# Attention, then two expert layers, on one core: a fixed order to the last pair, a spread gate chain, 32 products of constants

## Chip, cores and metric

One NeuronCore of a Trainium2 chip runs the whole program as one launch. The metric is the time of one execution in microseconds on the device. Three runs of the kernel before gave 632.25, 638.49 and 640.03 us; their median is 638.49 us.

## The reference, cut to what matters

```python
# q, k, v: 2 batches, 8 heads, 768 tokens, 64 per head; 4 sink keys; a window of 128
scores = scale * (q @ k.T)                      # kept: own 128-token window, and the sink keys
a = softmax(scores); x = (a @ v) as 1536 rows of 512
# first expert layer: 8 experts, the two best of each token, 512 -> 1024 -> 512
noisy = x @ w_gate + log1p(exp(x @ w_noise)) * noise
x = sum over the two best e of weight_e * (relu(x @ w1[e]) @ w2[e])
# second expert layer: 8 experts, the best of each token, with a bias by modality
out = prob_e * (relu(x @ w1b[e]) @ w2b[e])
```

## The kernel before, in words

**Attention.** The 1536 tokens are 12 tiles of 128 tokens. A tile has four pairs of heads, so there are 48 pairs, and the main loop (L1040) runs over pairs, j = 0 to 56, as a software pipeline written out by hand. In step j it issues the scores of pair j (`s_mm`, L406: 12 products of 128 columns in f16, 6 in the first tile of a batch, into one of two PSUM buffers named `s`), the row maxima of pair j-1 on DVE (`maxima`, L412 and L417), the exponentials of pair j-2 on ACT (L425), the turns of pair j-3 on TensorE (`pt_mm`, L431), and the products with V of pair j-7 (`pv`, L461, 8 products in f32). Other steps of a tile are put at a fixed number of pairs after its first one by a table (`put`, `fill`): the sink keys (L472, L503, L510, L516), the division by the row sums (`fin_x`, L535 and L537, which need the last products of the tile, L522), the split into two f16 halves (L547, L551), the turn of the row (L558 by DMA; for the last tile of a group, tiles 5 and 11, by eight products of TensorE, L562, and a copy on ACT, L563) and its gate logits (`lg_mm`, L568). The f16 splits of the first two experts' weights (L111 to L122) are put in between in the same way.

**Gating.** The tiles form two groups, 0 to 5 and 6 to 11. When the logits of a group are there, `gate_ops` (L574) makes a list of small operations, its gate chain (nearly all recorded as L609, the line of the helper `op`): noise, two best experts of each token (`max`, `max_index`), counts on TensorE (L647 to L650), ranks, then the slot lists: `lo` (128 x 1536), `ct` (128 x 1152), `ct` times the token numbers, and `place` (L702, 12 products). The chain of the first group ends in `ahead`, which gathers the rows of the first two experts' first blocks (L936) and appends their work to `todo` (four empty steps, then two turns L894, sixteen steps of the first layer L799, eight of the second L817, two that write rows). The chain of the second group ends in `gather1` (L763).

The chain's list holds marks, `BAR`. `drip` takes the next operation of the list unless it is a mark, and `tick` does so n times and then takes one mark away if it stands first. `maxima` drips `rate` operations at each of three places, `fin_x` two, and each step of the loop ends with a `tick` (L1082). So at most one section between marks is issued in a step:

```python
        rate[:], late_ticks, early_ticks = (DR, DR), TI if j < nu else PRM['TD'], 0
```

With DR 3 and TI 20, the first group's chain enters its list in step 38 and issues one whole section a step: step 39 has 29 operations (noise to the two best experts), step 45 has `lo`, `ct` and `ct` times tokens, step 46 `place`, step 47 the lists and `ahead`.

**Order.** Up to step MC the program order is the order on each engine (TensorE, DVE, ACT, POOL and the DMA queue of SP; `manual_schedule`, closed at L1042). After it a scheduler picks, for each engine, the next instruction at compile time from its own model of durations, with program order as priority. MC is 29, so 19 of the 48 pairs lie behind it. In program order `sink_p2` (L510) of a tile stands seven steps after the tile's first one, behind that step's scores, turns and products with V.

**Behind attention.** The work of `todo` is issued by a loop after the main loop, beside the second group's chain; then come the rest of experts 0 and 1 (L1411 to L1421, first product of `layer1(0)`: L799 with 288 columns), experts 2 to 7, and the second expert layer.

Of the kernel before, what the change touches and what calls it, by code (L numbers as in the profile page):

```python
# [1 line left out]
PRM = {"cuts": [0, 6, 12], "CP": 0, "BARS": 1, "DR": 3, "TI": 20, "TD": 30, "GW": 4, "JB": 50, "JN": 1, "TK": 4,  # L2
# [3 lines left out]
       "JP": 0, "XP": 0, "ptev": 5, "parts": 6, "max": 1, "finx": 10, "ptmm": 3, "exps": 2, "finsum": 9, "pv": 7,  # L6
# [33 lines left out]
def attention_moe_moe(ctx, tc, qk, v, n_sink, window, small, w1, w2, modality_id, modality_bias, w1b, w2b, out, CAP=416):  # L40
    nc = tc.nc
    V, A, G, T, S = nc.vector, nc.scalar, nc.gpsimd, nc.tensor, nc.sync
# [24 lines left out]
    cuts = PRM['cuts']  # L67
# [88 lines left out]
    sink = ps.tile([128, 512], FT, name="sink", bufs=1)  # L156
# [29 lines left out]
    ident = consts.tile([128, 128], HF, name="ident")  # L186
    tri = consts.tile([128, 128], HF, name="tri")
    ones = consts.tile([128, 128], HF, name="ones")
# [385 lines left out]
    def gate_ops(gi, ts, l):  # L574
# [31 lines left out]
        def op(f, *a, **kw):  # L606
            def run():
                with tc.high_priority(offset=CP):
                    f(*a, **kw)  # L609
            ops.append(run)  # L610
# [81 lines left out]
        def each(x, m):  # L692
            return x.rearrange("p c k -> p (c k)")[:, None, :].to_broadcast([128, m, 2 * n])

        op(V.tensor_tensor, lo, steps2[:, :, 0:2 * n], each(rh[:, 0], 128), op=OP.is_equal)
        op(V.tensor_tensor, ct, steps2[:, 0:NCOL, 0:2 * n], each(rh[:, 1], NCOL), op=OP.is_equal)
        op(V.tensor_tensor, ct, ct, each(tok1[:, t0:t0 + n], NCOL), op=OP.mult)
        bar()

# [229 lines left out]
    CP = PRM['CP']  # L929
# [69 lines left out]
    def tick(n):  # L999
        drip(n)  # L1000
        for c in chains:
            if c and c[0] is BAR:
                c.pop(0)
# [36 lines left out]
    for j in range(END):  # L1040
        if j == MC:
            man.close()  # L1042
        rate[:], late_ticks, early_ticks = (DR, DR), TI if j < nu else PRM['TD'], 0
        if early_ticks:
            tick(early_ticks)
        if j < nu:
            s_mm(*units[j])
        for h in range(2):
            k = j - PRM['finmm'] - 2 * h
            if k % 4 == 0 and 0 <= k // 4 < NT:  # L1050
                fin_mm(k // 4, h)
        k = j - PRM['ptev']
        if k % 2 == 0 and 0 <= k < nu:
            pt_ev(units[k][0], units[k][1] // 2)
        k = j - PRM['parts']
        if k % 2 == 0 and 0 <= k < nu:
            pt_parts(units[k][0], units[k][1] // 2)
        k = j - PRM['max']
        if 0 <= k < nu:
            maxima(*units[k])  # L1060
        for h in range(2):
            k = j - PRM['finx'] - 2 * h
            if k % 4 == 0 and 0 <= k // 4 < NT:
                fin_x(k // 4, h)
        k = j - PRM['ptmm']
        if 0 <= k < nu:
            pt_mm(*units[k])
        k = j - PRM['exps']
        if 0 <= k < nu:
            exps(*units[k])  # L1070
        for h in range(2):
            k = j - PRM['finsum'] - 2 * h
            if k % 4 == 0 and 0 <= k // 4 < NT:
                fin_sum(k // 4, h)
        k = j - PRM['pv']
        if 0 <= k < nu:
            pv(*units[k])
        if j >= JOBS:
            for _ in range(JN):
                step()  # L1080
        filled(j)
        tick(late_ticks)  # L1082
    ov = consts.tile([1, 2, E + 1], I32, name="ov")
    ovf = consts.tile([1, 2, E + 1], FT, name="ovf")
    at.close()
# [298 lines left out]
    j = END  # L1384
# [350 lines left out]
```

## Time and profile before

| | |
|---|---|
| three runs | 632.25, 638.49, 640.03 us; median 638.49 |
| the profiled execution | 641.03 us, its span 639.3 us |
| TensorE busy | 584.5 us (91%), mean granted clock 0.936 |
| DVE, ACT, POOL busy | 378.7 (59%), 301.8 (47%), 247.3 us (39%) |
| HBM | 142 GB/s over the span |

Times in the trace are microseconds from the start of the span. A granted clock of 1.00 is 2.4 GHz, one of 0.50 is 1.2 GHz. An instruction is named by its engine and by its line (L406 is line 406 of the kernel before).

### The profile page before, as it was taken

Reading aid. Unit: us, or ns where it says so; the run is one execution under the profiler, and the core shown is the slowest. Engines: PE = TensorE matmul, PEld = TensorE weight load, DVE = VectorE, ACT = ScalarE, POOL = GpSimd, SP = SyncE. Lnnn points to the kernel's source line nnn. Section 1 sums busy time; section 2 is a strip of 40 time slices with the busy share of each in tenths; the row PEclk is TensorE's granted clock in tenths of the full one; section 3 lists DMA queues with packets and bytes.
Section 4 is the critical chain, followed back from the end, with each engine's and each line's share of the span. In section 5 each row is a group of like instructions: output and inputs, shape, how many; then the busy total and the mean of one; then the engine's idle time right before and its main releaser. Section 6 shows DMA issues by size and latency. Waiting matters only on the chain. (4 is left out here: it accounts for less than half of the span.)

```text
span 639.3 us, 13126 instructions
## 1 busy us (share of the span) xinstructions
PE 584.5 (91%) x4764; PEld 407.5 (64%) x4764; DVE 378.7 (59%) x1036; ACT 301.8 (47%) x656; POOL 247.3 (39%) x274
## 2 busy tenths in 40 slices
PE   5699989799989999999999999999999697989982
PEld 4699888688867765555555555555545573755761
DVE  8799957934835848464747563356686572473420
ACT  6469857743234847454647463233452341452210
POOL 6577754432141354243341606042312381262210
PEclk9789968857899999999999999999999899889988
DMA  6778975447028578477584506017619865489320
GB/s 211 226 227 218 268 213 149 102 133 246 19 81 210 207 237 261 124 248 175 177 247 166 124 3 154 9 59 277 194 69 338 249 157 134 149 275 215 105 66 9
DMA packets 101048, 107.61 MB, mean 168 GB/s; under 512 B 62579, under 2 KB 65939, under 8 KB 100950
## 3 DMA queue, kind: packets, MB, share of 16 engines
q1 hardware_dynamic: 90102, 76.06, 42.9%
q0 software_dynamic: 9792, 28.26, 13.1%
q10 hardware_dynamic: 1056, 2.10, 0.9%
q8 instruction: 47, 0.77, 0.5%
q14 instruction: 51, 0.42, 0.2%
HBM read 76.03 MB, written 14.74 MB: 142 GB/s over the span
## 5 line engine op out<-in xcount | busy, mean ns | idle before, releaser
L799 PEld LDWEIGHTS <-w1s 128*128 128x128 f16 x1632 | 149.5, 102 | 85.6 <-issue 17.3
L799 PE MATMUL pp<-xtt,w1s 128*128 128x416 f16 (+2 forms) x864 | 152.3, 332 | 1.8 <-issue 1.0
L817 PE MATMUL pp<-hh,w2s 128*128 128x416 f16 (+2 forms) x960 | 141.4, 307 | 0.7 <-DVE hh L802 0.6
L817 PEld LDWEIGHTS <-w2s 128*128 128x128 f16 x960 | 87.7, 99 | 50.1 <-issue 1.0
L751 POOL DMA_INDIRECT yrow<-xga,ids x34 | 36.7, 1079 | 123.7 <-ACT xga L876 118.7
L825 DVE SCALAR_TENSOR_TENSOR yt<-pp,yt 64x416 f16<-64x416 f32 (+1 forms) x64 | 35.5, 555 | 65.2 <-ACT yt L823 58.4
L801 ACT ACTIVATE hh<-pp 128x416 f16<-128x416 f32 (+3 forms) x87 | 38.5, 461 | 57.8 <-PE pp L799 50.5
L802 DVE SCALAR_TENSOR_TENSOR hh<-pp,hh 128x416 f16<-128x416 f32 (+3 forms) x87 | 44.4, 518 | 32.3 <-ACT hh L801 22.7
L823 ACT ACTIVATE yt<-pp 64x416 f16<-64x416 f32 (+1 forms) x64 | 31.0, 485 | 68.1 <-PE pp L817 61.4
L122 DVE SCALAR_TENSOR_TENSOR w1s<-wf,w1s 128x1024 f16<-128x1024 f32 (+1 forms) x49 | 54.3, 1119 | 13.5 <-ACT w1s L115 10.0
L1539 PEld LDWEIGHTS <-hh 128*128 128x128 f16 x336 | 32.6, 98 | 37.9
L122 DVE SCALAR_TENSOR_TENSOR w2s<-wf,w2s 128x1024 f16<-128x1024 f32 (+1 forms) x43 | 52.6, 1262 | 3.3 <-ACT w2s L115 2.8
L461 PE MATMUL po<-vf,ptm 128*128 128x65 f32 x320 | 53.1, 319 | 0.6 <-issue 0.4
L1539 PE MATMUL po<-w2s,hh 128*128 128x512 f16 x240 | 52.8, 379 | 0.0
L461 PEld LDWEIGHTS po<-vf,ptm 128*128 128x128 f32 x320 | 51.2, 241 | 1.9 <-issue 1.2
L115 ACT ACTIVATE w1s<-wf 128x1024 f16<-128x1024 f32 (+1 forms) x51 | 45.6, 924 | 10.6 <-DMA wf<-in_moe_w_dram 5.0
L406 PEld LDWEIGHTS <-w2s 128*128 128x128 f16 x528 | 39.2, 113 | 14.2 <-issue 6.0
L115 ACT ACTIVATE w2s<-wf 128x1024 f16<-128x1024 f32 (+1 forms) x52 | 46.4, 918 | 0.9 <-remote 0.6
L763 POOL DMA_INDIRECT xg<-xrow,idg x30 | 30.2, 1008 | 29.0 <-DVE dst L609 20.1
L802 DVE SCALAR_TENSOR_TENSOR hh<-ph,hh 128x256 f16<-128x256 f32 (+1 forms) x48 | 17.2, 377 | 38.7 <-ACT hh L801 35.8
L406 PE MATMUL s<-w1s,w2s 128*128 128x128 f16 x264 | 31.4, 258 | 7.7 <-DVE w1s L348 5.4
L801 ACT ACTIVATE hh<-ph 128x256 f16<-128x256 f32 (+1 forms) x48 | 15.7, 347 | 46.7 <-PE ph L799 43.4
(304 smaller groups left out, 832.2 us busy)
## 6 DMA issues: line engine op xcount, KB each, us to landing
wf<-in_moe_w_dram SPq DMA_DIRECT2D x44, 1024.0 KB
w1s<-in_qk_dram SPq DMA_DIRECT2D x12, 512.0 KB
vf<-in_v_dram SPq DMA_DIRECT2D x12, 260.0 KB
xrow<-xr SPq DMA_DIRECT2D x12, 256.0 KB
w2s<-xga SPq DMA_DIRECT2D x22, 128.0 KB
wf<-in_moe_w_dram ACTq DMA_DIRECT2D x2, 1024.0 KB
yrow<-xga,ids POOLq DMA_INDIRECT x34
xtt<-xg SPq DMA_TRANSPOSE x31
```

Source lines behind the costliest of these rows:

```text
L115: A.activation(t[:, 0][:, o[0], o[1]], i, AF.Copy, scale=1.0 if v else SW)
L122: V.scalar_tensor_tensor(t[:, 1][:, o[0], o[1]], i, SW, h, op0=OP.mult, op1=OP.subtract)
L406: T.matmul(PS[t, p][:, c, j], head(t, a, 2 * p + j), KH[t - c][:, b, p // 2 * 2 + j], start=(j + a + b + c == 0), stop=(a > 0 and c == n - ...
L461: T.matmul(o[:, 2 * pp + j], x[:, 2 * pp + j], VV[t - c][:, 2 * p + j], start=(pp + j + c == 0), stop=(i == 0 and j + pp == 2), skip_group ...
L751: return G.indirect_dma_start(out=dst, out_offset=bass.IndirectOffsetOnAxis(ap=idx, axis=0), in_=src, in_offset=None, bounds_check=n - 1, ...
L799: ordered(1, T.matmul(p[:, :n], wa[:, a, d, fs], x[:, c * KD + d, r], start=(k_ == 0), stop=(k_ == len(passes) - 1)))
L801: A.activation(hh[:, 0, f, q], p[:, :n], AF.Relu)
L802: V.scalar_tensor_tensor(hh[:, 1, f, q], p[:, :n], 0.0, hh[:, 0, f, q], op0=OP.max, op1=OP.subtract)
L817: ordered(2, T.matmul(p[:, :n], wt[:, a, f, dd], hh[:, c, f, q], start=(k_ == 0), stop=(k_ == len(passes) - 1)))
L823: A.activation(y[s, 2 * d + x, r], p[s, :n], AF.Copy, scale=z)
L825: V.scalar_tensor_tensor(y[hs[1 - x], 2 * d + x, r], p[s, :n], z, y[s, 2 * d + x, r], op0=OP.mult, op1=OP.subtract)
L1539: T.matmul(p[:m], hh[:, c, f, o:o + m], wb[:, a, f], start=(f == 0 and k_ == 0), stop=(f == KF - 1 and k_ == 2))
```

## The change

Three parameters change: DR from 3 to 1, TI from 20 to 3, and MC from 29 to 48. Two marks are added between the three large operations of the first group's chain; the second group's chain, the last one, gets none there. Thirty-two products of two constants are issued at the end of step 47, into columns of the tile `sink` that nothing reads.

```diff
-PRM = {... "DR": 3, "TI": 20, ...
-       "MC": 29, ...
+PRM = {... "DR": 1, "TI": 3, ...
+       "MC": 48, ...
...
         op(V.tensor_tensor, lo, steps2[:, :, 0:2 * n], each(rh[:, 0], 128), op=OP.is_equal)
+        bar(gi < len(groups) - 1)
         op(V.tensor_tensor, ct, steps2[:, 0:NCOL, 0:2 * n], each(rh[:, 1], NCOL), op=OP.is_equal)
+        bar(gi < len(groups) - 1)
         op(V.tensor_tensor, ct, ct, each(tok1[:, t0:t0 + n], NCOL), op=OP.mult)
         bar()
...
         filled(j)
         tick(late_ticks)
+        if j == nu - 1:
+
+            for _ in range(32):
+                T.matmul(sink[:, 384:512], ones, ident, start=True, stop=True)
```

With one operation at each of the three places of `maxima` and three in the `tick`, a step issues six operations of the chain, eight where `fin_x` stands (every second step). Counted through the list: the section of 29 takes steps 40 to 44, the next three sections steps 45, 46 and 47, the product of the totals step 48, the ranks step 49 (behind the last pair the `tick` has 30 operations), `lo`, `ct` and the product with the tokens steps 50, 51 and 52, `place` 53, and the lists with `ahead` 54.

## Rows read from the trace of the kernel before

**Rows 1.** The page's 40 slices: granted TensorE clock in tenths of full speed
```profile
PEclk9789968857899999999999999999999899889988
```
**Rows 2.** Windows by stage: stretch, length, busy us (instructions) by engine, clock, DMA
```profile
67.96:83.28 15.32, 13.35 (x181) 12.02 (x180) 12.94 (x55) 12.46 (x39) 11.54 (x13) 1.00 1.07 296
83.28:102.03 18.75, 18.75 (x158) 17.44 (x157) 8.93 (x42) 9.29 (x30) 7.06 (x9) 0.54 0.68 165
102.03:119.72 17.69, 16.09 (x205) 13.97 (x204) 17.57 (x85) 13.61 (x39) 11.97 (x16) 1.00 0.40 113
119.72:125.23 5.51, 3.16 (x26) 2.68 (x27) 5.51 (x12) 4.41 (x11) 1.44 (x2) 0.93 0.73 183
125.23:146.76 21.53, 21.53 (x133) 19.17 (x130) 9.85 (x35) 9.37 (x23) 7.16 (x9) 0.50 0.43 118
146.76:185.44 38.68, 33.53 (x525) 31.51 (x525) 22.21 (x103) 12.75 (x47) 8.86 (x8) 0.89 0.36 113
```
**Rows 3.** Windows, L406 alone: the score products, 12 to a pair
```profile
67.96:83.28 15.32, 5.96 (x84) 4.97 (x83) 1.00 1.07 296
83.28:102.03 18.75, 7.20 (x60) 6.52 (x60) 0.54 0.68 165
102.03:119.72 17.69, 5.17 (x72) 4.28 (x72) 1.00 0.40 113
```
**Rows 4.** Windows: two stretches at half clock, and one at full
```profile
83.50:100.57 17.07, 17.07 (x146) 15.98 (x143) 7.67 (x34) 8.02 (x25) 6.84 (x9) 0.50 0.65 150
124.46:151.77 27.31, 27.31 (x203) 24.79 (x202) 14.58 (x46) 11.78 (x32) 9.79 (x11) 0.50 0.49 142
...
36.00:83.50 47.50, 44.92 (x580) 40.35 (x577) 42.99 (x164) 39.50 (x120) 36.90 (x46) 1.00 0.88 242
```
**Rows 5.** Timeline of TensorE before the first fall: start, length, instruction, [idle before]
```profile
83.11 0.24 PE L510 MATMUL sink<-ident,sks 128*64 128x128 f16 x1 [1.40 <-POOL sks L503]
83.29 0.23 PE L406 MATMUL s<-w1s,w2s 128*128 128x128 f16 x1
```
**Rows 6.** Timeline of TensorE around the second fall
```profile
117.82 1.00 PE L461 MATMUL po<-vf,ptm 128*128 128x65 f32 x8
...
119.73 0.84 PE L406 MATMUL s<-w2s 128*128 128x128 f16 x12 [0.41 <-DVE mx L417]
...
123.14 2.28 PE L702 MATMUL misc<-ct,lo 128*128 128x96 f16 x12 [2.34 <-DVE ct L609]
125.24 1.46 PE L406 MATMUL s<-w2s 128*128 128x128 f16 x12
126.50 1.91 PE L461 MATMUL po<-vf,ptm 128*128 128x65 f32 x8
```
**Rows 7.** Timeline of DVE there
```profile
119.60 0.99 DVE L609 TENSOR_TENSOR ct<-steps,rh 128x1152 f16<-128x1152 f16 x1
...
121.38 1.71 DVE L609 TENSOR_TENSOR ct<-ct,tok 128x1152 f16<-128x1152 f16 x1
```
**Rows 8.** Timeline of TensorE, the turn and the logits of tile 5
```profile
93.76 1.01 PE L562 MATMUL s<-ident,xr 128*128 128x128 f16 x8
...
96.30 0.51 PE L568 MATMUL misc<-wg,xt 128*128 128x16 f16 x12
```
**Rows 9.** Timeline of ACT, the copy between them
```profile
94.81 1.01 ACT L563 COPY xt<-s 128x1024 f16<-128x1024 f16 x1 [2.58 <-PE s L562]
```
**Rows 10.** Groups of DVE, 100 to 130 us: first chain; count, busy us, mean ns
```profile
L609 DVE SCALAR_TENSOR_TENSOR gw<-gw 128x48 f32<-128x48 f32 x8 | 4.4, 553 | 0.0
```
**Rows 11.** The same group, 158 to 174 us: second chain
```profile
L609 DVE SCALAR_TENSOR_TENSOR gw<-gw 128x48 f32<-128x48 f32 x8 | 1.6, 205 | 0.2
```
**Rows 12.** Timeline of TensorE, the second chain's last count
```profile
165.66 0.17 PE L650 MATMUL misc<-acum,ones 128*128 128x8 f16 x1
```
**Rows 13.** Timeline of POOL: first gathers of the first and of the second chain
```profile
126.36 1.21 POOL L936 DMA_INDIRECT xga<-xrow,idga  x1 [3.89 <-DVE mx L417]
...
173.28 0.99 POOL L763 DMA_INDIRECT xg<-xrow,idg  x1 [20.12 <-DVE dst L609]
```

More of the change, by code (lines that the diff above doesn't have):

```diff
@@ L1 @@
 import math
-PRM = {"cuts": [0, 6, 12], "CP": 0, "BARS": 1, "DR": 3, "TI": 20, "TD": 30, "GW": 4, "JB": 50, "JN": 1, "TK": 4,
[1 row of a table removed]
+PRM = {"cuts": [0, 6, 12], "CP": 0, "BARS": 1, "DR": 1, "TI": 3, "TD": 30, "GW": 4, "JB": 50, "JN": 1, "TK": 4,
[1 row of a table added]
        1, "direct": 1, "OT": 2, "S3": 0, "SK": 1, "SL": 0, "LS": 2, "L0": 2, "LN": 3, "LW": 12, "EN": 9, "xs": 128,
```

2 rows, old and new, of the table PRM are left out of this document.

## The prediction

> **What bounds the kernel now.** I read the slices of the granted clock first, because TensorE is the busiest engine and its clock is what varies: the row is 8 or 9 nearly everywhere, but 6 in the sixth slice (80 to 96 us) and 5 in the ninth (128 to 144) [rows 1]. Then the windows. Two long stretches run at 0.50, that is 1.2 GHz: 83.50 to 100.57 and 124.46 to 151.77 [rows 4]. In both TensorE is busy all the time (17.07 of 17.07, 27.31 of 27.31), so the lower clock there is paid in full: at 2.4 GHz the same products would take about half, 8.5 and 13.7 us less.
>
> The stage windows put this against the work [rows 2], and the score products alone count the pairs [rows 3]: 84 products are seven pairs, 60 five, 72 six. Pairs 28 to 34 take 15.32 us at full clock, 2.19 each. Pairs 35 to 39 take 18.75, 3.75 each, at a mean clock of 0.54. Pairs 40 to 45 take 17.69, 2.95 each, at full clock again; there DVE is busy 17.57 of 17.69, since the first group's gate chain runs on it. Pair 46 with what follows takes 5.51, and then come 21.53 us of remaining products with V, turns and logits at 0.50.
>
> What TensorE did before the falls: ahead of the first it waited 1.40 us for POOL with L510 at the head of its line, though the scores of pair 35 (83.29) stood ready behind it [rows 5]; ahead of the second it waited 2.34 us with `place` at the head [rows 6], while DVE made `ct` and `lo` in one piece from 119.60 to 123.01 [rows 7]. Both orders are the scheduler's. A busy TensorE alone did not bring the clock back: through the drain it stayed low, and it rose at 151.77, five microseconds after the first of the first-layer products, dense f16, at 146.77 [rows 2, 4].
>
> **The change part by part.**
>
> *Fixed order, first half.* In program order L510 stands behind its step's scores, so I take out the 1.40 us: pair 35 starts at 81.9. Pairs 35 to 39 then go at the full-clock pace, 5 x 2.19 = 10.95. The fixed order adds one wait of its own, at step 37: the eight turns of tile 5, the copy on ACT and the twelve logit products stand directly behind one another in TensorE's line, while now other products lie between [rows 8]. The copy takes 1.01 us [rows 9]; queued behind the waiting logits are the sink products and the scores of pair 38, for which DVE and ACT wait in turn. The turn also takes one of the two `s` buffers. Bounds 1.0 and 2.5 us; I take 1.5, nearest to the copy itself. Pair 40: 81.9 + 10.95 + 1.5 = 94.3, before 102.04, so 7.7 us earlier.
>
> *Spread chain, steps 38 to 47.* The 29 DVE operations of the second section and the counts still fall beside the pairs; the ranks, the three large operations and `place` go behind pair 47. So four pairs cost what pairs 40 to 45 cost before, 2.95, and three, with three to eight short operations each, between 2.19 and 2.95: I take 2.6. Pair 47 starts at 94.3 + 11.8 + 7.8 = 113.9, before 125.24, so 11.3 us earlier. Bounds for the seven pairs: 15.3 (all at 2.19) and 20.7 (all at 2.95). The marks cost no time themselves. On SP the DMA of the gate values only moves behind the last pair.
>
> One row speaks against spreading. The eight gate operations of 128 x 48 took 553 ns each while POOL worked beside them, 205 ns in the second chain, where it hardly did [rows 10, 11]: some 2.8 us in all. The Trainium skill says in "SBUF — State Buffer", section "SBUF: two separate sides", that a DVE operation with two inputs from SBUF and a GpSimd operation share a pair of ports, and that whoever comes second stands still for the whole instruction of the other. By that rule each operation that is put between other work can meet a POOL instruction; by the row the mean is 0.35 us longer, half of the price of one such stop (1.71 against 0.99 us for two passes of one size) [rows 7]. My sum keeps the row; the rule's case is the fourth rival.
>
> *The 32 products.* They have the form of the score products, whose twelve last 0.84 us at full clock and 1.46 at half [rows 6]. Without the tail of the last one (0.23) that is some 0.055 or 0.11 us each, so 1.8 or 3.5 us of TensorE's line, with the tail of step 47 ahead of them. Nothing hides this: the seven pairs' products with V wait behind them. I take 1.8. Below nothing is possible too: being dense f16 they may keep or bring back the clock, which is counted next. What reads `sink` in step 48 may wait for them; its answer is wanted only by the sums behind several products with V.
>
> *The drain.* From pair 47's scores to the first product of the `ahead` work: 21.53 us at 0.50, TensorE never idle [rows 2]. At full clock half, 10.8; eight products with V take 1.00 instead of 1.91 [rows 6]. The trace shows no stretch with these products alone at full clock, and `place` with its 2.28 us for 12 products now falls inside. So bounds 10.8 and 21.5, and I take the middle, 16: full clock at first, the lower one later. The `ahead` work starts at 113.9 + 1.8 + 16 = 131.7, before 146.77.
>
> *Is the first group's list in time?* From the totals on, the chain now runs behind pair 47. The second chain needed 7.6 us from its last count (165.66) to its first gather (173.28) [rows 12, 13], between other work. From 113.9 + about 3 for the step and the 32 products that gives a gather at 124.5, against 126.36 before [rows 13]; before, the turns of the gathered rows followed 10 us later, behind other products, so 131.7 still covers it. If not, TensorE stands idle and the delay is added.
>
> *Behind it.* 146.77 to 185.45 is 38.68 us with TensorE busy 33.53 [rows 2]; the work, the second chain and its gathers all start from the end of the drain, so I carry the gain through unchanged, and through the expert layers, where the clock row stays at 9 to the 31st slice.
>
> **Sum.** 146.77 - 131.7 = 15.1 us off the profiled execution of 641.03 (span 639.3): 625.9. That execution lies 2.5 us above the median of the three runs, 638.49, so I forecast 623. With the bounds added up: best 81.9 + 10.95 + 1.0 + 15.3 + 1.8 + 10.8 = 121.8, 25 us off, 613; worst 81.9 + 10.95 + 2.5 + 20.7 + 3.5 + 21.5 = 141.1, 5.7 us off, 633. The forecast's own range is 616 to 631.
>
> **Rivals.**
> 1. *Full clock throughout.* The 32 products and the fixed order keep 2.4 GHz through the drain. For: the level held from 36 to 83.5 us, mostly in fixed order, with TensorE busy 44.92 of 47.50 [rows 4]. Against: no stretch with f32 products alone at that level. Time 613.
> 2. *The clock falls at tile 5's turn.* The new wait of 1 to 2.5 us is as long as the two that preceded the falls [rows 5, 6]. If it stays low for five pairs as before, 5 x (3.75 - 2.19) = 7.8 us go: 631; for all ten pairs 15.6, of which the 32 dense products give some back in the drain. I take 631.
> 3. *Nothing gained: the waits move.* The scheduler's order avoided waits that the fixed order has at other places, and the drain falls to half right behind the 32 products. Time 638. Against: the same stretch of 47.50 us, which kept its clock [rows 4].
> 4. *DVE against POOL.* Sixteen operations of the first sections have two SBUF inputs. With the mean stretch of the eight (553 - 205 = 0.35) they lose 5.6 us, which the pace of 2.95 holds already; if each waits 0.72, by which the two passes over `ct` differ (1.71 and 0.99) [rows 7], 11.5: 5.9 more, 629. This is the case of the SBUF page's rule.
> 5. *Slower.* The fixed order puts chain operations ahead of the maxima in DVE's line, TensorE waits for each pair, the clock falls at pair 38 (88.5) and stays: nine pairs at 5.3, nearest to the 5.51 of pair 46, end at 136.2; with 3.5 and 21.5 the `ahead` work starts at 161, 14.4 late: 653. It decides from about 5.1 us a pair (at 3.7 it is a draw). Against: pairs 40 to 45 held 2.95 with the same section on DVE.
>
> **How the numbers follow.** Chances: forecast 0.48, full clock 0.12, tile 5's turn 0.20, DVE against POOL 0.06, waits move 0.08, slower 0.06. The range 612 to 636 holds forecast, rivals 1, 2 and 4, and leaves out the rest and the tails. A measurement of this kernel can tell about 2%, 12.8 us, from no change: faster means under 625.7. Of the forecast's own range some two thirds lie below that (0.32), with rival 1 (0.12) and a little of rival 2 (0.04) that is 0.48; slower 0.06; within 2% the other 0.46.
>
> **What would show it.** Right: L510 of tile 7 behind pair 35's scores with no wait; granted clock 1.00 from 36 to about 115; pair 47's scores near 114, the 32 products behind them in 1.8 us; `place` behind them; first `ahead` product near 132, L799 with 288 columns near 170. Wrong: a gap of over 2 us at step 37 and 0.50 behind it; pairs 40 to 47 slower than 2.95; a drain still of 21 us; or TensorE idle for the gathered rows of L936.

## The result, and the profile after

| | before | after |
|---|---|---|
| median of 20 runs each, in the order before, after, before ... | 638.2 us (632.16 to 645.78) | 641.49 us (637.62 to 650.5) |
| ratio, 95% interval | | 1.008 [1.0056, 1.0105] |
| the profiled execution, its span | 641.03, 639.3 us | 640.64, 638.8 us |
| TensorE busy, mean clock | 584.5 us, 0.936 | 576.2 us, 0.945 |

Nothing was gained; by the ratio the change costs some 5 us of 638, about 1%. The gain was forecast at 15 us, in the stretch from pair 28 to the `ahead` work. One caution for all that follows: the ratios leave out the longer runs of each kernel (over 1.5% above its fastest), and the profiled executions of the kernel before that is shown above, and of e2, g2, g3, h3 and h4 below, are among the longer ones, so their stage times show what happened within them, and differences between kernels are read from the others and from the ratios. First the page of the kernel after, its span and the slices of the clock; the row that answers is [rows 1].

```profile
span 638.8 us, 13198 instructions
...
PEclk9789989958989999999999999999999899989987
```

The slice at 80 to 96 us has gone from 6 to 8, but the ninth (128 to 144) stands at 5 as before. The windows by stage of the kernel after (columns as in [rows 2]; pairs 28 to 34, 35 to 39, 40 to 46, then pair 47 with the drain, then `ahead` up to `layer1(0)` with 288 columns):

```profile
67.54:85.05 17.51, 15.11 (x179) 14.34 (x179) 13.34 (x54) 13.54 (x38) 11.18 (x11) 0.81 1.10 293
85.05:99.94 14.89, 13.46 (x162) 12.30 (x161) 9.48 (x39) 14.14 (x41) 10.75 (x14) 0.89 0.61 153
99.94:118.62 18.68, 15.70 (x213) 14.26 (x213) 18.11 (x89) 11.72 (x35) 9.30 (x13) 1.00 0.55 169
118.62:147.31 28.69, 22.96 (x205) 19.63 (x202) 15.52 (x55) 12.98 (x34) 17.20 (x16) 0.67 0.70 186
147.31:185.47 38.16, 32.08 (x510) 29.47 (x508) 19.05 (x98) 12.97 (x45) 4.90 (x5) 0.93 0.16 50
```

Pair 40 is 2.1 us earlier than before (99.95 against 102.04) and pair 47 6.6 us earlier (118.63 against 125.24). Then the drain takes 28.69 us where it took 21.53 [rows 2], and its first `ahead` product comes at 147.32, before at 146.77. What was won in the pairs against this execution is lost behind them, to half a microsecond.

The timeline of TensorE in the kernel after (start, length, instruction, idle time before it; lines from L702 on are three higher than before, and L1089 is the 32 products):

```profile
77.85 0.49 PE L568 MATMUL misc<-wg,xt 128*128 128x16 f16 x12 [2.40 <-DMA xt<-xr]
...
93.51 0.46 PE L568 MATMUL misc<-wg,xt 128*128 128x16 f16 x12 [1.21 <-ACT xt L563]
...
118.63 0.83 PE L406 MATMUL s<-w2s 128*128 128x128 f16 x12
...
121.39 1.96 PE L1089 MATMUL sink<-ident,ones 128*128 128x128 f16 x32
...
128.76 0.31 PE L510 MATMUL sink<-ident,sks 128*64 128x128 f16 x1 [0.98 <-POOL sks L503]
...
133.16 1.60 PE L705 MATMUL misc<-ct,lo 128*128 128x96 f16 x8
134.58 3.54 PE L461 MATMUL po<-vf,ptm 128*128 128x65 f32 x16
...
139.16 0.54 PE L705 MATMUL misc<-ct,lo 128*128 128x96 f16 x2
...
144.63 1.03 PE L897 MATMUL pp<-ident,xga 128*128 128x128 f16 x8 [4.11 <-DMA xga<-xrow,idga]
...
147.32 0.74 PE L802 MATMUL pp<-xta,w1s 128*128 128x128 f16 x5
```

Two things to see. In the pairs, the logits of a tile (L568) wait twice at the head of TensorE's line for the turned rows, for a DMA and for the copy on ACT. In the drain, `place` (L705) is no longer one piece of 2.28 us [rows 6] but is cut up among products with V from 133.16 to 139.70, and the turns of the gathered rows (L897) then find TensorE idle for 4.11 us. Windows of the kernel after over the stretches at half clock:

```profile
77.25:84.25 7.00, 6.40 (x69) 6.40 (x70) 3.45 (x16) 5.41 (x16) 4.60 (x6) 0.51 1.06 345
94.50:97.75 3.25, 3.25 (x25) 3.25 (x23) 1.16 (x6) 3.16 (x14) 3.17 (x5) 0.50 0.53 134
128.50:149.00 20.50, 15.48 (x107) 13.22 (x108) 5.72 (x20) 5.16 (x12) 8.51 (x8) 0.50 0.61 151
```

The clock fell around each wait for the turned rows, and around the 0.98 us wait for POOL at 128.76. In place of the long stretch before, 83.50 to 100.57 [rows 4], there are two, of 7.00 and 3.25 us; the one of the drain is still there, 20.50 instead of 27.31.

### The profile page after: what moved, and what is told of

Read it like the earlier page. It is cut to its first block, busy times and chain, and to the rows that moved or that the text cites. A ratio compares the mean times of both kernels' runs of the same rounds, so it can differ in the third digit from the quotient of the medians.

```text
span 638.8 us, 13198 instructions
## 1 busy us (share of the span) xinstructions
PE 576.2 (90%) x4796; PEld 400.5 (63%) x4796; DVE 374.0 (59%) x1036; ACT 302.8 (47%) x656; POOL 248.4 (39%) x274
## 5 line engine op out<-in xcount | busy, mean ns | idle before, releaser
L802 PEld LDWEIGHTS <-w1s 128*128 128x128 f16 x1632 | 147.8, 101 | 87.3 <-issue 14.7
L406 PEld LDWEIGHTS <-w2s 128*128 128x128 f16 x528 | 38.4, 112 | 13.6 <-issue 5.0
L461 PE MATMUL po<-vf,ptm 128*128 128x65 f32 x320 | 46.0, 294 | 0.0
L461 PEld LDWEIGHTS po<-vf,ptm 128*128 128x128 f32 x320 | 44.6, 216 | 0.4 <-issue 0.2
L406 PE MATMUL s<-w1s,w2s 128*128 128x128 f16 x264 | 30.5, 251 | 7.6 <-DVE w1s L348 5.4
L804 ACT ACTIVATE hh<-ph 128x256 f16<-128x256 f32 (+1 forms) x48 | 15.6, 348 | 44.8 <-PE ph L802 41.6
```

What stands on the lines that cost most here:

```text
L406: T.matmul(PS[t, p][:, c, j], head(t, a, 2 * p + j), KH[t - c][:, b, p // 2 * 2 + j], start=(j + a + b + c == 0), stop=(a > 0 and c == n - ...
L461: T.matmul(o[:, 2 * pp + j], x[:, 2 * pp + j], VV[t - c][:, 2 * p + j], start=(pp + j + c == 0), stop=(i == 0 and j + pp == 2), skip_group ...
L802: ordered(1, T.matmul(p[:, :n], wa[:, a, d, fs], x[:, c * KD + d, r], start=(k_ == 0), stop=(k_ == len(passes) - 1)))
L804: A.activation(hh[:, 0, f, q], p[:, :n], AF.Relu)
```

## The experiments

All runs have a profile of one execution. This table sums up the stages of each, from the first score product of pair 28, 40 and 47 to the first product of the `ahead` work, and the ratio of times to the kernel before, measured beside it on the same chip (intervals of 95%). The two rows of before are the same program; so are those of after, and e4 and h4. One program's ratio differs from one measurement to the next (after: 1.008, 1.0151, 1.017; e4 and h4: 0.9836, 0.9904), so kernels that were not measured beside one another aren't told apart here by less than 0.01. The stages aren't the whole time either: from the first `ahead` product to the end these executions took from 485.5 us (h1) to 501.2 (e2).

| kernel | 28 to 40 | 40 to 47 | drain | sum | ratio |
|---|---|---|---|---|---|
| before | 34.07 | 23.20 | 21.53 | 78.80 | |
| before, again | 26.47 | 23.22 | 21.54 | 71.23 | |
| after | 32.40 | 18.68 | 28.69 | 79.77 | 1.008 [1.0056, 1.0105] |
| after, again | 31.75 | 25.57 | 32.23 | 89.54 | 1.0151 [1.01, 1.0201] |
| after, a third time | 32.69 | 18.68 | 28.67 | 80.04 | 1.017 [1.0094, 1.0245] |
| e1: without the products | 32.52 | 18.66 | 27.84 | 79.02 | 1.0085 [1.0042, 1.0129] |
| e2: fixed order alone | 35.55 | 30.58 | 23.10 | 89.24 | 1.0191 [1.0131, 1.0251] |
| e3: spread chain alone | 28.07 | 17.01 | 27.57 | 72.65 | 0.9991 [0.9956, 1.0027] |
| e4: products alone | 28.09 | 23.84 | 13.11 | 65.04 | 0.9836 [0.9773, 0.9899] |
| f1: list earlier | 34.06 | 18.55 | 25.32 | 77.93 | 1.0139 [1.0057, 1.022] |
| f2: logits later | 29.56 | 18.75 | 24.25 | 72.56 | 1.0102 [1.0013, 1.0191] |
| f3: spread and products | 26.47 | 17.00 | 30.59 | 74.06 | 1.0045 [0.9999, 1.009] |
| f4: f1 and f2 | 31.63 | 20.91 | 26.91 | 79.45 | 1.0223 [1.0147, 1.03] |
| g1: products along the drain | 32.13 | 17.11 | 36.29 | 85.53 | 1.0311 [1.0251, 1.0372] |
| g2: fixed order to the drain | 35.46 | 23.77 | 35.09 | 94.32 | 1.0262 [1.0211, 1.0313] |
| h1: turns a step later | 25.94 | 23.03 | 28.30 | 77.27 | 1.0149 [1.0097, 1.0201] |
| h3: e4, order fixed to 35 | 30.89 | 25.26 | 12.56 | 68.71 | 0.9981 [0.9936, 1.0026] |
| h4: e4 again | 29.28 | 24.37 | 12.93 | 66.58 | 0.9904 [0.9857, 0.9951] |

### The parts of the change, one at a time (e1 to e4)

**e1**, the change without its products:

```diff
-        if j == nu - 1:
-            for _ in range(32): T.matmul(sink[:, 384:512], ones, ident, ...)
```

> The changed kernel (641.5 us) without the 32 products. Theory (the first group's list is late: the chain, moved behind pair 47, delays the gather of the ahead work, and TensorE stands idle for it): the product of the totals stands right behind pair 47 instead of behind 32 products, the gather comes about 2 us earlier than 141.0, time 639 to 640. Rival A (the clock alone: the drain of f32 products falls to half whatever is put ahead of it, and the products only put that off): the fall comes one stage earlier, pair 47 unchanged near 118.6, drain longer, 643 to 646. Rival B (the fixed order's own waits eat the gain): no difference beyond the 1.8 us, 640.

Measured 1.0085, the change itself 1.008, and each stage within a microsecond of the change's. In this setting the 32 products do nothing that the intervals can tell: their 1.96 us are neither paid for nor earned. They don't put the fall off either: without them the clock falls 9.7 us behind pair 47's scores (near 128.1), with them 9.9. The gather comes at 139.84, 1.2 us earlier. Of the three cases written down, rival B fits.

**e2**, the kernel before with the order fixed to the last pair:

```diff
-       "MC": 29,
+       "MC": 48,
```

> The kernel before with the order fixed to pair 47 (MC 48) and nothing else: the chain keeps its whole sections (29 operations in step 39, the three large ones in step 45, the lists in step 47). Theory: the list is there by pair 47, the gather comes near 124 instead of 141, no idle TensorE ahead of the turns of the gathered rows, and the earlier end of the pairs is kept: 630 to 634. Rival A: the drain is at half clock all the same, 636 to 639. Rival B: 29 operations in one step hold up the maxima by 6 to 10 us, pairs 39 to 41 slow, clock falls, 642 or more.

Measured 1.0191. Windows (pairs 40 to 46, then the drain), and the row of TensorE at pair 40:

```profile
100.55:131.13 30.58, 29.29 (x225) 26.84 (x226) 22.31 (x104) 16.04 (x43) 11.68 (x13) 0.50 0.40 114
131.13:154.23 23.10, 23.10 (x137) 19.93 (x138) 11.29 (x30) 6.92 (x20) 11.17 (x13) 0.50 0.54 146
```
```profile
100.56 0.27 PE L406 MATMUL s<-w2s 128*128 128x128 f16 x1 [2.94 <-DVE gw L609]
```

Operations of the section of 29 stand on DVE in front of each of the two maxima of a pair (three from 96.45 on ahead of the one at 98.66, three more ahead of the one at 100.06), and the scores of pair 40 wait 2.94 us. From 99.5 on the clock is 0.50 in this execution, through pairs and drain. TensorE idles for only 1.29 of the 30.58 us of these pairs, so they are slow by the clock and not by a wait for each pair. The order is the one that the fifth rival describes, and rival B came: slower. The gathers are in time (133.45, 2.3 us behind pair 47, and no wait for them), and the drain is at half clock all the same. The change, with its chain spread, has one wait over 1 us in pairs 40 to 46, of 1.28 us, and a clock of 1.00 there; g3 below is an execution of the same program in which the clock fell there too.

**e3**, the spread chain alone, in the scheduler's order:

```diff
-       "MC": 48,
+       "MC": 29,
...
-                T.matmul(sink[:, 384:512], ones, ident, ...)
```

> The kernel before with the chain spread (DR 1, TI 3, the two marks) and nothing else: order fixed to pair 28 only, no products. Theory: the list is late here too, since its operations have a low place in program order and come behind pair 47: the gather falls behind 135, 642 to 646. Rival A: the place product no longer waits with the pairs, so the second fall comes later, 634 to 637. Rival B (the loss is the fixed order's): no change, 638.

Measured 0.9991, no difference: rival B. The gather is late, near the theory's 135 (133.54, 21 us behind pair 47), but the time of 642 to 646 didn't come. Windows, pairs 40 to 46 and the drain:

```profile
95.31:112.32 17.01, 15.95 (x207) 14.29 (x207) 17.01 (x83) 13.74 (x40) 11.93 (x16) 1.00 0.48 123
112.32:139.89 27.57, 21.80 (x187) 18.39 (x187) 20.29 (x55) 13.44 (x35) 13.02 (x14) 0.67 0.72 197
```

Pairs 40 to 46 take 17.01 us, some 6 less than in either execution of before (23.20, 23.22), and the drain takes 27.57, some 6 more than theirs (21.53, 21.54). The spread moves 6 us from one stage to the next.

**e4**, the 32 products alone, in the kernel before:

```diff
         tick(late_ticks)
+        if j == nu - 1:
+            for _ in range(32): T.matmul(sink[:, 384:512], ones, ident, ...)
```

> The kernel before with the 32 products and nothing else. Theory: they cost their 1.8 to 3.5 us of TensorE's line, or up to half of it where they bring the clock back for a while: 637 to 641. Rival A (the clock decides): they bring the granted clock back to 1.00 in the drain, which goes from 21.5 to some 15 us: 632 to 634.

Measured 0.9836, about 10 us faster: rival A. The medians of all its 12 runs and of all 29 of the kernel before are 633.22 and 637.30 us, 4 us apart, so the size of the gain is less sure than that there is one. Windows of the three stages:

```profile
68.84:96.93 28.09, 26.11 (x338) 24.04 (x337) 21.39 (x94) 21.39 (x68) 18.99 (x21) 0.94 0.92 253
96.93:120.77 23.84, 21.16 (x263) 18.45 (x263) 23.69 (x103) 18.90 (x50) 13.43 (x17) 1.00 0.53 149
120.77:133.88 13.11, 12.26 (x135) 10.73 (x131) 9.26 (x32) 8.33 (x22) 8.04 (x9) 1.00 0.81 162
```

The drain runs at 1.00 and takes 13.11 us instead of 21.53. Its first gather starts at 121.26, half a microsecond behind pair 47's scores (120.78), so the turns find their rows. In the change, the first gather starts at 141.03, 22.4 us behind pair 47.

### What holds the drain up (f1 to f4, g1, g2)

Two suspects for the change: the list that comes late, and the turns' waits with the clock that falls around them. **f1** gives the list back its place, **f2** moves the logits of a tile one step later, **f3** leaves the scheduler its order, **f4** is f1 and f2 together. Each edits the kernel after:

```diff
f1:
-       "DR": 1, "TI": 3
+       "DR": 2, "TI": 6
-        bar(gi < len(groups) - 1)        (both)
f2:
-       "lgmm": 19, "lg": 20
+       "lgmm": 20, "lg": 21
f3:
-       "MC": 48
+       "MC": 29
```

> The changed kernel (641.5 us) with a middle rate, DR 2 and TI 6, and without the two new marks: the section of 29 takes steps 39 to 41, the three large operations come in step 47, place in 48, the lists in 49 instead of 54; order and products as in the change. Theory (the late list is the main loss): gathers near 128 instead of 141, no wait for them, drain under 20 us instead of 28, time 632 to 635. Rival A (the drain is slow because of its clock): gathers earlier but the drain still 25 us or more, 640. Rival B (the fixed order's waits ahead of pair 40 are the whole loss): drain shorter, but pair 47 later by as much because of the faster chain, 641.

> The changed kernel with the gate logits of all tiles but 5 and 11 one step later (lgmm 20, lg 21), so that the turn of tile 3 by DMA has 2 us more before TensorE waits for it at step 31. Rival B (the fixed order's waits): the wait of 2.4 us and the half clock of 7 us behind it go, some 5 us, pair 47 near 113.5, and all that follows 4 to 5 us earlier: 636 to 637. Theory: pair 47 is earlier, but the late list follows the pairs only in part, 638 to 640.

> The changed kernel with the order fixed to pair 28 only (MC 29), so the spread chain and the products without the fixed order. If the fixed order is the loss and the products are the gain (spread alone 0.999, products alone 0.984 of before): 626 to 630. If the late list, which the spread brings in any order, takes what the products give: 634 to 638, with gathers still near 133.

> Both edits, the earlier list and the later logits, under the order fixed to pair 47 with the 32 products. If the two losses are the list and the wait at step 31, they add up: 627 to 631. If one of them covers the other: as the better of the two alone, 632 to 637.

f1 measured 1.0139. Its windows, pairs 40 to 46 and the drain, and the first gather in the timeline of POOL:

```profile
100.96:119.51 18.55, 15.65 (x213) 14.22 (x214) 17.97 (x95) 11.48 (x34) 8.91 (x11) 1.00 0.49 146
119.51:144.83 25.32, 24.91 (x194) 21.01 (x194) 15.81 (x46) 13.70 (x35) 12.19 (x14) 0.67 0.83 219
```
```profile
131.87 1.22 POOL L937 DMA_INDIRECT xga<-xrow,idga  x1 [0.18 <-issue]
```

The gather comes 9 us earlier than in the change and TensorE is hardly idle in the drain (24.91 of 25.32), yet the drain takes 25.32 at a clock of 0.67: the late list alone is not it, as rival A had it. With the list in time, the same stretch is filled with work at half clock.

f2 measured 1.0102. Windows of its three stages:

```profile
65.97:95.53 29.56, 26.86 (x351) 24.35 (x350) 22.30 (x84) 26.69 (x77) 20.49 (x23) 0.94 0.93 249
95.53:114.28 18.75, 15.70 (x213) 14.26 (x213) 18.18 (x90) 11.63 (x35) 9.55 (x14) 1.00 0.52 167
114.28:138.53 24.25, 19.01 (x216) 16.89 (x214) 15.80 (x55) 13.14 (x35) 16.12 (x16) 0.84 0.78 222
```

With the logits a step later pairs 28 to 40 take 29.56 us instead of 32.40, and the drain idles 5.24 us (of which 4.62 before the turns), waiting for the list. f2 takes out the wait of tile 3 alone; the one for the copy of tile 5 stays (1.10 us, at 89.09). Its interval overlaps the change's, so the gain of 3 us in the pairs is seen in the profile and not in the time. f3 measured 1.0045: in the scheduler's order the pairs are fast (26.47 and 17.00) and the drain is slow (30.59), with the 32 products in it. In kind that is the second case written down for it. f4, at 1.0223, is no better than either of its halves, which neither of its two cases had; its clock fell at 89.5 for 20 us, and again at 127.

**g1** strews the products along the drain, eight in each of nine steps (72 in all); **g2** fixes the order through the drain and leaves the 32 at one place:

```diff
g1 and g2:
-       "MC": 48
+       "MC": 56
g1:
-        if j == nu - 1:
-            for _ in range(32):
+        if nu - 1 <= j < nu + 8:
+            for _ in range(8):
```

> The changed kernel with the order fixed through the drain (MC 56) and the products of constants spread over it: eight behind each of the steps 47 to 55, 72 in all, instead of 32 behind step 47. Theory now (the drain is slow because its f32 products do not hold 2.4 GHz; the 32 products only put the fall off by some 7 us): the granted clock stays at 1.00 from pair 47 to the first-layer products, the drain takes 15 to 18 us with the 4 us of the 72 products in it, instead of 28, and the time is 8 to 11 us below the changed kernel on the same chip. Rival (the late list sets the end of the drain): the clock stays up, TensorE idles for the gathers, drain 24 us or more, 2 to 4 us below. Rival (the fixed order's waits): same as the changed kernel or slower.

> The control for the run beside it: the changed kernel with the order fixed through the drain (MC 56) and its 32 products where they are. Theory: half clock from some 7 us behind pair 47 on as in the changed kernel, drain 25 to 30 us, time within 3 us of the changed kernel. If the scheduler's order in the drain is what is bad (place cut up between products with V, 133 to 140), place now takes 2.3 us in one piece, the gathers come by 135, and it is 4 to 6 us below.

Measured 1.0311 and 1.0262, the slowest of all, against 1.0151 for the change beside them (g3). In g1 the second eight products waited for a copy of the tile they write into, though it reads other columns:

```profile
123.96 0.61 PE L1089 MATMUL sink<-ident,ones 128*128 128x128 f16 x8 [1.70 <-DVE skt L516]
```

The clock fell at 126 and again at 132.75, and the gathers came at 141.35, with TensorE idle for 5.94 us. So g1 answers nothing on whether strewn products would hold the clock; a version with a tile of its own for them wasn't tried. In g2's execution `place` was in one piece again (144.67 to 146.96), but the gathers stand 23 us behind pair 47 (147.96 against 124.63), no nearer than in the change.

### The same program again, and the turns (g3, g4, h1, h2)

> The changed kernel itself, as the reference for the two runs beside it on the same chip, and a second profiled execution. If the clock's falls at step 31 and behind pair 47 belong to the order of the work, they are at the same places again (near 77 and 128 us), for some 7 and 20 us; if they are chance, they move. Time 1.008 of before.

> The kernel before itself, for a second profiled execution. If the 17 us at half clock from 83.5 on, which the forecast took out, are what every execution pays, they are there again; if that execution was an unlucky one, the clock is back after one stage of some 3.4 us, as in the runs of the spread alone and of the products alone, pair 38 starts near 93 instead of 97, and the forecast's first term was too large by 4 us. The drain at half clock should be there again.

g4 is the kernel before, with no edit, in one more profiled execution (628.36 us). Windows of its stages, and of the one stretch at half clock up to 143:

```profile
69.08:95.55 26.47, 24.50 (x338) 22.43 (x337) 21.96 (x94) 21.36 (x68) 19.11 (x21) 1.00 0.99 269
95.55:118.77 23.22, 19.25 (x231) 16.65 (x231) 23.22 (x101) 18.27 (x49) 13.44 (x17) 0.93 0.52 151
118.77:140.31 21.54, 21.54 (x133) 19.18 (x130) 9.85 (x35) 9.38 (x23) 7.16 (x9) 0.50 0.42 118
```
```profile
115.75:143.00 27.25, 26.31 (x178) 23.58 (x178) 14.83 (x50) 12.34 (x32) 7.74 (x11) 0.50 0.45 124
```

The first fall, 17 us long in [rows 4], isn't there: pairs 28 to 40 take 26.47 us at 1.00. Pair 40 starts at 95.56, which is near to what was forecast for the kernel after (94.3). The drain is the same as before to a hundredth, 21.54 us at 0.50 and never idle. So the 17 us of the first fall belonged to that one execution, the second fall to the program. The wait that stands ahead of the first fall in [rows 5] is in g4 too, with no fall behind it, in its timeline of TensorE:

```profile
84.23 0.24 PE L510 MATMUL sink<-ident,sks 128*64 128x128 f16 x1 [1.40 <-POOL sks L503]
```

Six of the executions have the scheduler's order at this place, and with it this wait, of 1.40 or 1.41 us. Half clock follows for 17.07 us in the kernel before, for 3.4 in e3, e4 and h4, and not at all in g4 and f3. So the wait alone doesn't decide; what does isn't shown.

g3, the kernel after with no edit, measured 1.0151: on this chip too it isn't faster than before. Near step 31 and behind pair 47 its clock falls again (74.3 for 3.4 us, 135.8 for 20.5), but the second time 14.0 us behind pair 47's scores instead of 9.9. A long fall is new, from 101.6 to 129.0, around a wait of 1.65 us for the maxima (102.29), and pairs 40 to 46 take 25.57 us instead of 18.68. So the falls belong to the order of the work only in part.

**h1** moves the logits of all tiles, those of the last one of a group among them; **h2** is the kernel after once more, on the same chip.

```diff
h1:
-       "lgmm": 19, "lg": 20, "lgmme": 17, "lge": 18
+       "lgmm": 20, "lg": 21, "lgmme": 18, "lge": 19
```

> The changed kernel with the gate logits of every tile one step behind where they stood (lgmm 20, lg 21, and for tiles 5 and 11 lgmme 18, lge 19), so that in the fixed order no logits stand at the head of TensorE's line while a turn, by DMA or on ACT, is under way; the first group's chain starts one step later. Theory (in the fixed order these waits, steps 31, 35 and 37, make the clock fall in the pairs, and that is the order's cost): no fall between 36 us and pair 47, pair 47 near 112 in every execution, 6 to 9 us below the changed kernel beside it. Rival (the drain alone decides): pairs earlier, but the time within 3 us of the changed kernel.

> The changed kernel again, as the reference on the same chip for the run before it: waits at steps 31, 35 and 37 as in its two other executions, 1.005 to 1.015 of before.

h2 repeats the first execution of the change nearly to the microsecond (32.69, 18.68, 28.67). h1 has none of the waits for turned rows, and pairs 28 to 39 take 25.94 us at 1.00, against 32.69 in h2. But the time is 1.0149 against 1.017, intervals that overlap, as the rival had it. What is late next is DVE, in the timeline of TensorE in h1:

```profile
103.43 0.23 PE L406 MATMUL s<-w2s 128*128 128x128 f16 x1 [2.24 <-DVE mx L417]
...
108.37 0.83 PE L406 MATMUL s<-w2s 128*128 128x128 f16 x12 [2.38 <-DVE m L609]
```

Behind the second of these waits the clock falls, from 109.6 to 116.4, against the theory of no fall up to pair 47. Pairs 40 to 46 take 23.03 us there, as much as in the kernel before, and the drain 28.30.

### A version meant to beat both (h3, h4)

**h3** is e4 with the order fixed to pair 35 and the logits a step later; **h4** is e4 again, unchanged.

```diff
h3, on e4:
-       "MC": 29, "lgmm": 19, "lg": 20
+       "MC": 36, "lgmm": 20, "lg": 21
```

> A version meant to beat both: the kernel before with the 32 products, the order fixed to pair 35 (MC 36) so that L510 does not wait for POOL ahead of pair 35's scores, and the logits one step later (lgmm 20, lg 21) so that they do not wait at steps 31 and 35. Theory: no fall near 84 us, the drain at full clock as with the products alone: 2 to 4 us below the products alone, 0.975 to 0.982 of before. Rival (what follows pair 35 is ordered anew by the scheduler, and the products land elsewhere): as the products alone or slower.

> The kernel before with the 32 products alone, again, as the reference on the same chip for the run before it: 0.984 of before, the drain from pair 47 to the first ahead product some 12 us at full clock.

h4 measured 0.9904 [0.9857, 0.9951]: the products alone are faster than the kernel before a second time, by about 6 us (4 by the medians of all runs, 625.74 and 630.04). h3 measured 0.9981: with the order fixed to pair 35 no gain can be told, though its profiled execution has the short drain (12.56). The fall that it was to take out is there, 6.8 us from 83.6 on, around a wait of 1.80 us for POOL at other products (83.39); whether the gain went there isn't settled. What the products do can be followed within h4's execution, in the timeline of TensorE around `place`, and in the window at half clock:

```profile
121.39 1.17 PE L1086 MATMUL sink<-ident,ones 128*128 128x128 f16 x18
123.90 2.27 PE L702 MATMUL misc<-ct,lo 128*128 128x96 f16 x12 [1.34 <-DVE ct L609]
125.98 1.35 PE L1086 MATMUL sink<-ident,ones 128*128 128x128 f16 x11
127.13 1.16 PE L406 MATMUL s<-w2s 128*128 128x128 f16 x9
```
```profile
125.50:129.00 3.50, 3.50 (x30) 3.40 (x29) 1.91 (x12) 2.00 (x6) 1.60 (x2) 0.52 0.03 7
```

The scheduler puts them on both sides of the wait for `ct`: eighteen ahead of it, which shorten the wait from 2.34 us [rows 6] to 1.34, and eleven behind `place`, followed by the scores of pair 47. The clock fell at 125.50 and was back at 129.00. In the kernel before, the fall at the same place lasted 27.31 us [rows 4], and 27.25 in g4, with products with V behind the scores. In e4, with the same order and a wait of 1.33, it didn't fall there at all. Which of the products it takes, those ahead of the wait or those behind it, was not tried apart, nor the order fixed to pair 47 with the products and without the spread chain.

## Why the prediction was wrong

The forecast was 623 us and the first `ahead` product at 131.7; it came at 147.32, 15.6 us late, and the time is 641.49. Two terms of the sum failed: the pairs up to 40 under the fixed order, and the drain with its products. The miss by its steps:

| step | forecast | measured | adds |
|---|---|---|---|
| pair 40 starts | 94.3 | 99.95 | +5.65 |
| pairs 40 to 47 | 19.6 | 18.68 | -0.9 |
| products and drain | 17.8 | 28.69 | +10.9 |
| first `ahead` product | 131.7 | 147.32 | +15.6 |
| from there to `layer1(0)`, 288 columns | 38.68 | 38.16 | -0.5 |

**The fixed order's first half: failed.** L510 of tile 7 stands behind its step's scores without a wait, as forecast, and the long fall is gone. But "pairs 35 to 39 then go at the full-clock pace" fell, and so did "the fixed order adds one wait of its own, at step 37". That wait came, at 1.21 us, within its bounds of 1.0 to 2.5. The prediction did not see the other: the logits of tile 3 in step 31, 2.40 us for a DMA. The timeline of SP's queue in the kernel after has that turn:

```profile
67.45 4.74 SPq L558 DMA_TRANSPOSE xt<-xr  x1
```

From its issue to the logits at 77.85 are 10.40 us, and TensorE stood ready for them after 8.0 (at 75.45); the DMA engines were at a share of 1.10 in that stretch. Before, the scheduler took these logits at 78.51, with no wait. An estimate from the windows: the two stretches at half clock hold 9.65 us of busy TensorE, half of it lost, 4.8; with the two waits, 2.40 and 1.21, that is 8.4 us, of which the forecast held 1.5, so 6.9 too much. The stage came out 6.1 us longer than the forecast from the same pair 28 (32.40 against 26.3). e1, h2 and g3 repeat it (32.52, 32.69, 31.75), f2 and h1, with the logits later, shorten it (29.56, 25.94); the six executions in the scheduler's order lie between 26.47 and 34.07. The second rival, a fall at tile 5's turn, came true as a mechanism, but for 3.25 us, not for five pairs.

**The spread chain, pairs 40 to 47: right.** 18.68 us, forecast 19.6, bounds 15.3 to 20.7, and 18.68 again in h2; in g3 a fall of the clock made it 25.57. TensorE waited over 1 us once, 1.28 us for the maxima (108.30).

**DVE against POOL: as the sum had it.** The eight operations of [rows 10] went down to 222 ns in the mean, so spreading did not make them longer. The rule of the Trainium skill, "SBUF — State Buffer", section "SBUF: two separate sides", that one of the two stands still for the whole instruction of the other, is to be seen in single rows. Timelines of DVE and of POOL in the kernel after:

```profile
105.66 1.16 DVE L609 TENSOR_TENSOR gw<-gw,sml 128x48 f32<-128x48 f32 x1
106.85 0.21 DVE L609 TENSOR_TENSOR gw<-gw,lg 128x48 f32<-128x48 f32 x1
```
```profile
105.59 1.16 POOL L551 TENSOR_TENSOR xr<-x,xr 128x512 f16<-128x512 f32 x1 [2.56 <-DVE xr L545]
```

Of two operations of one size the one beside POOL's row ends where that ends, within 0.07 us. The trace agrees with the rule; only two of the spread operations of this size were held for so long (the other at 100.77, 1.15 us), so the fourth rival was off.

**The 32 products: right in price, wrong in effect.** 1.96 us, forecast 1.8. The forecast let them keep the clock up in the drain ("full clock at first, the lower one later"). The clock did stay at 1.00 for 5 us behind them, as it did without them in e1, and fell at 128.50, around a wait of 0.98 us for POOL that the forecast did not have. From there to the turns at 144.63 the longest run of f16 products is 1.60 us (`place`, 133.16). By e1 their effect here is nil within the intervals; in e4 and h4 the drain of the kernel before is 8 to 9 us shorter with them (13.11 and 12.93 against 21.53), where the scheduler puts them around the wait. The drain at full clock, which no trace had shown, lies between the bounds of 10.8 and 21.5.

**The drain: failed.** The sum had 1.8 and 16 for products and drain, and they took 28.69. An estimate from the trace: TensorE idles 5.73 us of it, 4.11 of them ahead of the turns, and from 128.56 to 147.31 it works 13.79 us at half clock, half of which, 6.9, is the price of the clock. Without both it would be 16.1. So the lower clock came earlier and cost more than the middle between the bounds allowed for, and the idle time, which the sum put at nothing, was added.

**The list in time: failed.** The gather was forecast at 124.5 from the second chain's 7.6 us [rows 12, 13]; it came at 141.03. Timelines of DVE and TensorE before, in the second chain:

```profile
169.01 0.75 DVE L609 TENSOR_TENSOR ct<-ct,tok 128x1152 f16<-128x1152 f16 x1
```
```profile
169.82 2.28 PE L702 MATMUL misc<-ct,lo 128*128 128x96 f16 x12 [0.56 <-DVE ct L609]
```

The timelines of DVE and POOL in the kernel after:

```profile
129.45 0.98 DVE L609 TENSOR_TENSOR ct<-ct,tok 128x1152 f16<-128x1152 f16 x1
...
139.74 0.26 DVE L609 TENSOR_TENSOR lst<-misc,lst 128x96 f32<-128x96 f32 x1 [4.58 <-PE misc L705]
```
```profile
141.03 1.22 POOL L939 DMA_INDIRECT xga<-xrow,idga  x1 [4.86 <-DVE dst L609]
```

From the totals on TensorE, behind the 32 products at 123.18, it is 7.25 us to the end of `ct` (130.43), 2.73 until TensorE takes up `place`, 6.54 for `place` in pieces among products with V at half clock, and 1.33 to the gather: 17.85. In the second chain the same four parts were 4.10, 0.06, 2.28 and 1.18 us. TensorE was busy there too (7.06 of 7.62 us), but at a clock of 0.93 and with `place` in one piece, and POOL hardly worked; here the clock is 0.65, `place` is cut up, and POOL works 7.83 us of the 17.85. The step of the prediction carried the price of one stretch over to another with a lower clock and another order. Of the 16.5 us that the gather is late, this is 10.2; the rest is pair 47, 4.7 us late, and step 47 with the products, 4.5 us instead of 3. Its alternative, "if not, TensorE stands idle and the delay is added", came true with 4.11 us. f1 shows that this is not the whole of it.

**The carry: right.** 38.16 us, forecast 38.68.

**The base: failed in part.** The forecast took all of the first fall as a gain to be had. g4 shows the kernel before without it, 6.5 us ahead at pair 40, and with the very wait of 1.40 us that the forecast took out as what stood ahead of the fall. The median of the runs, 638.49, did not tell which kind of execution the profiled one was.

The third rival, "nothing gained: the waits move", at 638, was nearest in time and in kind, and had 0.08. What the experiments add is which part does what: the products alone gain, the order fixed alone loses (e2), and the spread moves 6 us from the pairs to the drain. Beside the spread the products gain nothing (drain 30.59 in f3, 27.57 without them in e3); that the late list is the reason is argued and not shown, since in f1, with the list earlier, the drain is at half clock too. How the lost time is shared between the turns' waits and the drain isn't settled: f2 takes one of the waits out, h1 both, and their times don't stand apart from the change's. Why the clock falls at one wait and not at another stays open.

## What to carry to other kernels

Look at two executions of a kernel before you count a fall of the clock as time to be won. An order fixed by hand turns each round trip through DMA or another engine into a wait at the head of the line, so its table must leave the slowest trip its time where the queues are fullest (here 10.4 us, with TensorE ready after 8.0). Work that is moved out of a bound stage needs cover where it lands. Dense products that are to hold the clock were worth something in this kernel directly before and behind the wait around which it fell, and nothing 5 us ahead of a stretch that had waits of its own.

## What the runs showed of the hardware that was not expected

- One program's executions differ, and in the profiles by where the clock falls: the 20 runs of before span 632.16 to 645.78 us, and two profiles of it differ by 7.6 us from pair 28 to 40 alone (34.07 and 26.47) for the same work.
- A TensorE that never idled stayed at 0.50: 21.53 and 21.54 us of the drain in two executions, with products of 65 columns in f32, and 27.31 us in one stretch. In h4, eleven products of 128 columns in f16 and the scores of a pair stood within the 3.5 us before it rose.
- The clock fell around waits of 0.98 and 1.21 us (at 128.50 and 94.50), no longer than others around which it didn't (1.28 us at 108.30), and one wait of 1.40 us at the same place of the same order had 17, 3.4 or no us of half clock behind it. Length alone doesn't tell.
- The 12 products of `place` take 2.27 us for 96 columns each at full clock (e4, 118.06), the 12 scores of 128 columns 0.84 [rows 6].
- Products into columns of a PSUM tile that nobody reads still waited for a reader of the tile, 1.70 us in g1. Whether that is the chip or the kernel's own tracking of whole tiles was not tried.
